# Windowed attention with global keys and a squared-ReLU MoE: attention cut into units that are placed between the steps of the MoE

## The chip, the cores and the metric

The kernel runs on one core of a Trainium2 chip. TensorE (PE; its weight loads are shown apart as PEld), VectorE (DVE), ScalarE (ACT), GpSimd (POOL) and SyncE (SP) each work through their own list of instructions in order and wait for each other by semaphores. DMA transfers are issued from POOL's and SP's lists and run beside them. The metric is device time in microseconds (us), the median of three runs.

## The reference

```python
# q, k, v: (4, 8, 768, 64), n_global = 8, n_local = 96; moe_w_in: (512, 2048), moe_w_out: (2048, 512)
scores = scale * np.matmul(q, k.transpose(0, 1, 3, 2))
rel = pos[:, None] - pos[None, :]
is_global = pos[None, :] < int(n_global)
is_local = (rel >= 0) & (rel < int(n_local))
keep = is_global | is_local
dist = np.where(is_global & ~is_local, float(n_local), np.abs(rel).astype(np.float32))
bias = -slopes[:, None, None] * dist[None, :, :]
scores = np.where(keep, scores + bias[None, :, :, :], -1000000000.0)
a = softmax(scores)          # over the keys
x = np.matmul(a, v)          # (4, 8, 768, 64), then laid out as 3072 tokens x 512
h = x @ w_in
r = np.maximum(h, 0.0)
out = (r * r) @ w_out        # (3072, 512), float32
```

A query of tile t (128 tokens) thus sees keys of its own tile, of the tile to the left, and the first eight keys of its batch.

## The kernel before

It has two stages, one after the other, and a scheduler of the tile framework orders each engine's list within them. All inputs are float32 in memory; POOL's DMA issues turn them into bfloat16 on the way.

*Attention* (L155 to L257) runs over 4 batches and 4 pairs of heads. For a pair, q and k of 768 tokens are loaded in four transfers (L164, L168; 128 partitions x 6 x 64 elements), transposed by PE in 128x128 blocks (L176, L181) and copied out of PSUM by DVE (L188, L189). For each head v is loaded (L198) and given a column of ones by POOL (L202). For each of six query tiles up to three 128x128 key blocks are multiplied (L218): the first tile of the batch for its global keys, the left tile and the own one. ACT takes the exponential of up to 384 columns (L228), DVE multiplies by a table of exponentiated biases, which is zero where a key is masked (L235), PE multiplies by v with its ones (L239: 64 outputs and the sum of the row), and DVE takes the reciprocal of the sum (L249) and scales (L250) into `x_sbuf`, which keeps all 3072 tokens.

*The MoE* (L259 to L318) starts when the attention pools are closed. It runs over 6 blocks of 512 tokens: PE transposes x (L278), DVE copies it (L284), and for each of 16 chunks of 128 hidden columns PE makes four matmuls of 512 columns (L290, stage 1), ACT the ReLU (L299), DVE the square (L301), PE four matmuls of 512 columns (L303, stage 2). ACT copies the sums out (L314), SP stores them (L315). Both weights come in one transfer each (L138, L143), issued ahead of q and k. [...]

Of the kernel before, what the change touches and what calls it, by code (L numbers as in the profile page):

```python
# [12 lines left out]
FP32 = mybir.dt.float32  # L14
BF16 = mybir.dt.bfloat16


@with_exitstack
def kernel(
# [26 lines left out]
    Act = mybir.ActivationFunctionType  # L46

    consts = ctx.enter_context(tc.tile_pool(name="consts", bufs=1))

    ident = consts.tile([128, 128], BF16)  # L50
    make_identity(nc, ident)

    def build_local_prebT(dst, offset):
        nc.gpsimd.iota(
            dst.bitcast(mybir.dt.int32),
            pattern=[[-1, 128]],
            base=-offset,
            channel_multiplier=1,
        )
# [31 lines left out]
    def build_prebT(offset, include_global, global_only, name):
        dst = consts.tile([128, 128], FP32, name=name, tag=name)
        if global_only:
            nc.gpsimd.memset(dst, float(-n_local))
            mask_globalT(dst)
        else:
            build_local_prebT(dst, offset)
            if include_global:
                gt = consts.tile([128, 128], FP32, name="gtT", tag="gtT")
                nc.gpsimd.memset(gt, float(-n_local))  # L100
                mask_globalT(gt)
                nc.vector.tensor_max(dst, dst, gt)
        return dst

    pbT_Br0 = build_prebT(0, True, False, "pbT_Br0")
    pbT_Ar128 = build_prebT(128, True, False, "pbT_Ar128")
    pbT_B = build_prebT(0, False, False, "pbT_B")
    pbT_G = build_prebT(0, False, True, "pbT_G")
    pbT_A = build_prebT(128, False, False, "pbT_A")

    pbT_cfg = [
        [pbT_Br0],
        [pbT_Ar128, pbT_B],
        [pbT_G, pbT_A, pbT_B],
    ]

    expBT = []
    for h in range(H):
        row = []
        for cfg in range(3):  # L120
            blocks = pbT_cfg[cfg]
            nb = len(blocks)
            eb = consts.tile(
                [128, nb * 128], BF16, name=f"eT_{h}_{cfg}", tag=f"eT_{h}_{cfg}"
            )
            for bi, pb in enumerate(blocks):
                nc.scalar.activation(
                    eb[:, bi * 128 : (bi + 1) * 128],
                    pb,
                    Act.Exp,  # L130
                    scale=float(slopes[h]),
                )
            row.append(eb)
        expBT.append(row)

    KM = d_model // 128
    w_in_sbuf = consts.tile([128, KM, d_ff], BF16)
    nc.gpsimd.dma_start(  # L138
        out=w_in_sbuf, in_=moe_w_in.rearrange("(km p) f -> p km f", p=128)
    )  # L140
    KF = d_ff // 128
    w_out_sbuf = consts.tile([128, KF, d_model], BF16)
    nc.gpsimd.dma_start(  # L143
        out=w_out_sbuf, in_=moe_w_out.rearrange("(kf p) f -> p kf f", p=128)
    )

    N_BT = B * N_ROW_TILES
    x_sbuf = consts.tile([128, N_BT, H, D], BF16)

    attn_ctx = ctx.enter_context(ExitStack())  # L150
    qkv_pool = attn_ctx.enter_context(tc.tile_pool(name="qkv", bufs=2))
    tqk = attn_ctx.enter_context(tc.tile_pool(name="tqk", bufs=2))
    work = attn_ctx.enter_context(tc.tile_pool(name="work", bufs=3))
    scalar_pool = attn_ctx.enter_context(tc.tile_pool(name="sc", bufs=4))
    psum_tr = attn_ctx.enter_context(tc.tile_pool(name="psumtr", bufs=1, space=bass.MemoryType.PSUM))  # L155
    psum_pool = attn_ctx.enter_context(tc.tile_pool(name="psum", bufs=3, space=bass.MemoryType.PSUM))
    psum_out = attn_ctx.enter_context(tc.tile_pool(name="psumo", bufs=3, space=bass.MemoryType.PSUM))

    for b in range(B):
        for kp in range(H // 2):  # L160
            q_b = qkv_pool.tile([128, N_ROW_TILES, 128], BF16, tag="q_b")
            k_b = qkv_pool.tile([128, N_ROW_TILES, 128], BF16, tag="k_b")
            for hh in range(2):
                nc.gpsimd.dma_start(  # L164
                    out=q_b[:, :, hh * D : (hh + 1) * D],
                    in_=q[b, 2 * kp + hh, :, :].rearrange("(t p) d -> p t d", p=128),
                )
                nc.gpsimd.dma_start(  # L168
                    out=k_b[:, :, hh * D : (hh + 1) * D],
                    in_=k[b, 2 * kp + hh, :, :].rearrange("(t p) d -> p t d", p=128),  # L170
                )
# [181 lines left out]
```

## Time and profile before

| | us |
|---|---|
| median of 3 runs | 407.82 (407.51 to 430.92) |
| span of the profiled execution | 406.0 |
| PE busy | 329.8 (81%) |
| DVE busy | 199.7 (49%) |
| ACT busy | 161.1 (40%) |
| POOL busy | 89.3 (22%) |

The span runs from the first to the last instruction of one profiled execution, whose own time is not listed apart from those of the runs. A busy time is the union of an engine's instructions; durations of matmuls are modelled from start to drain, so successive ones overlap, and what one costs in a row of them is the distance of their starts. Idle time counts only on the engine that the others wait for.

### The profile page before, as it was taken

What the parts mean: (1) busy time and instruction counts of PE and PEld (TensorE: products, weight loads), DVE (VectorE), ACT (ScalarE), POOL (GpSimd) and SP (SyncE); (2) the same over time, 40 slices, a digit from 0 to 9 for tenths busy, and PEclk for the clock granted to TensorE, in tenths of its full rate; (3) what the DMA queues carried; (4) which work ended last, traced back from release to release, by engine and by line L of the source; (5) the groups of instructions that cost most, each with busy time, mean ns of one, the idle gap of its engine ahead of it and who ended that gap; (6) DMA issues with size and microseconds to landing.
All of it is one profiled execution on the core that took longest, in us unless ns stands there. A gap on an engine that the chain in (4) does not pass through costs nothing.

```text
span 406.0 us, 5757 instructions
## 1 busy us (share of the span) xinstructions
PE 329.8 (81%) x1999; PEld 165.1 (41%) x2016; DVE 199.7 (49%) x712; ACT 161.1 (40%) x361; POOL 89.3 (22%) x158
## 2 busy tenths in 40 slices
PE   0008888888888888888897998999999999999991
PEld 0005544444555444444453334444434444434430
DVE  0004776776666777676763444335335335345240
ACT  6403444444544444443451334335235235235232
POOL 9316634544543443531100000000000000000000
PEclk9999999999999999999999999999999999999998
DMA  3999998899777879853310002001102002002002
GB/s 53 200 193 111 75 57 56 52 61 58 49 46 50 52 51 61 56 32 21 22 10 0 2 0 101 4 0 61 44 0 79 26 1 97 9 2 103 0 2 103
DMA packets 81341, 20.30 MB, mean 50 GB/s; under 512 B 75680, under 2 KB 77728, under 8 KB 81312
## 3 DMA queue, kind: packets, MB, share of 16 engines
q0 software_dynamic: 77856, 13.64, 42.6%
q1 hardware_dynamic: 3456, 6.29, 4.1%
q8 instruction: 16, 0.26, 0.3%
q14 instruction: 13, 0.11, 0.1%
HBM read 27.26 MB, written 6.29 MB: 83 GB/s over the span
## 4 chain that ended last, share of the span: by engine, by line
PE 73%; DVE 14%; DMA 6%; issue 2%; POOL 2%; ACT 2%; DVEq 0%; POOLq 0%; ACTq 0%
PE ps_out L303 21%; PE hT_ps L290 20%; PE sc_ps L218 15%; PE out_ps L239 9%; DMA q_b<-in_q_dram 5%; DVE attnT L235 4%; PE kT_ps L181 4%; PE qT_ps L176 4%; DVE x_sbuf L250 3%; DVE rsum L249 2%; DVE kT L189 2%; DVE xT L284 1%; DMA out_dram<-out_tile 1%; DVE h_sq L301 1%; ACT h_relu L299 1%
## 5 line engine op out<-in xcount | busy, mean ns | idle before, releaser
L228 ACT ACTIVATE esc<-sc_ps 128x384 bf16<-128x384 f32 (+1 forms) x192 | 81.1, 437 | 117.0 <-PE sc_ps L218 80.0
L301 DVE TENSOR_TENSOR h_sq<-h_relu 128x512 bf16<-128x512 f32 x96 | 66.3, 693 | 108.4 <-ACT h_relu L299 108.4
L299 ACT ACTIVATE h_relu<-hT_ps 128x512 f32<-128x512 f32 x96 | 57.1, 601 | 108.9 <-PE hT_ps L290 102.5
L290 PE MATMUL hT_ps<-xT,w_in_sbuf 128*128 128x512 bf16 x372 | 91.1, 386 | 4.3 <-DVE xT L284 3.1
L303 PE MATMUL ps_out<-w_out_sbuf,h_sq 128*128 128x512 bf16 x379 | 90.3, 381 | 4.2 <-DVE h_sq L301 3.7
L218 PE MATMUL sc_ps<-qT,kT 64*128 64x128 bf16 x480 | 81.5, 301 | 5.8 <-DVE kT L189 5.8
L239 PE MATMUL out_ps<-vS,attnT 128*128 128x65 bf16 x480 | 62.6, 244 | 23.6 <-DVE attnT L235 21.3
L235 DVE TENSOR_TENSOR attnT<-esc,eT 128x384 bf16<-128x384 bf16 (+1 forms) x192 | 59.7, 311 | 4.3 <-ACT esc L228 1.0
L290 PEld LDWEIGHTS <-w_in_sbuf 128*128 128x128 bf16 x384 | 37.6, 99 | 51.2 <-issue 4.7
L249 DVE RECIPROCAL rsum<-out_ps 128x1 f32<-128x1 f32 x192 | 31.9, 166 | 51.7 <-PE out_ps L239 50.6
L239 PEld LDWEIGHTS <-attnT 128*128 128x128 bf16 x480 | 36.9, 123 | 47.7 <-DVE attnT L235 41.4
L303 PEld LDWEIGHTS <-h_sq 128*128 128x128 bf16 x384 | 31.9, 98 | 57.6 <-DVE h_sq L301 28.1
L218 PEld LDWEIGHTS <-kT 64*128 64x128 bf16 x480 | 39.9, 121 | 25.4 <-DVE kT L189 8.3
L250 DVE TENSOR_SCALAR x_sbuf<-out_ps,rsum 128x64 bf16<-128x64 f32 x192 | 49.3, 277 | 0.1
L176 PE MATMUL qT_ps<-ident,q_b 128*128 128x128 bf16 x96 | 18.5, 302 | 31.3 <-DMA q_b<-in_q_dram 31.0
L168 POOL DMA_DIRECT2D k_b<-in_k_dram x32 | 26.3, 824 | 35.1 <-PE out_ps L239 22.1
L198 POOL DMA_DIRECT2D vS<-in_v_dram x32 | 26.5, 829 | 16.0 <-POOL vS L202 7.7
L164 POOL DMA_DIRECT2D q_b<-in_q_dram x32 | 26.3, 824 | 16.1 <-PE out_ps L239 9.4
L176 PEld LDWEIGHTS <-q_b 128*128 128x128 bf16 x96 | 8.0, 120 | 38.6 <-issue 37.1
L188 DVE COPY qT<-qT_ps 128x768 bf16<-128x768 bf16 x16 | 8.7, 542 | 28.0 <-PE qT_ps L176 28.0
L181 PE MATMUL kT_ps<-ident,k_b 128*128 128x128 bf16 x96 | 22.1, 296 | 0.0
L314 ACT COPY out_tile<-ps_out 128x512 f32<-128x512 f32 x24 | 13.1, 590 | 12.8 <-PE ps_out L303 11.1
(42 smaller groups left out, 69.1 us busy)
## 6 DMA issues: line engine op xcount, KB each, us to landing
out_dram<-out_tile SPq DMA_DIRECT2D x24, 256.0 KB, 2.0
q_b<-in_q_dram POOLq DMA_DIRECT2D x32, 96.0 KB, 3.3
k_b<-in_k_dram POOLq DMA_DIRECT2D x32, 96.0 KB, 3.2
vS<-in_v_dram POOLq DMA_DIRECT2D x32, 96.0 KB, 3.2
w_in_sbuf<-in_moe_w_in_dram POOLq DMA_DIRECT2D x1, 2048.0 KB, 12.8
w_out_sbuf<-in_moe_w_out_dram POOLq DMA_DIRECT2D x1, 2048.0 KB, 22.5
```

Of the source, the lines that this page charges most:

```text
L176: nc.tensor.transpose(out=qT_ps[:, t * 128 : (t + 1) * 128], in_=q_b[:, t, :], identity=ident,)
L181: nc.tensor.transpose(out=kT_ps[:, t * 128 : (t + 1) * 128], in_=k_b[:, t, :], identity=ident,)
L218: nc.tensor.matmul(out=sc_ps[:, bi * 128 : (bi + 1) * 128], lhsT=kT[:, kb * 128 : (kb + 1) * 128], rhs=qT[:, r : r + 128], start=True, sto ...
L228: nc.scalar.activation(out=esc[:, :ncols], in_=sc_ps[:, :ncols], func=Act.Exp, scale=scale,)
L235: nc.vector.tensor_mul(attnT[:, :ncols], esc[:, :ncols], expBT[h][cfg])
L239: nc.tensor.matmul(out=out_ps, lhsT=attnT[:, 128 * bi : 128 * (bi + 1)], rhs=vS[:, kb, :], start=(bi == 0), stop=(bi == nblk - 1), skip_gr ...
L249: nc.vector.reciprocal(rsum, out_ps[:, D : D + 1])
L250: nc.vector.tensor_scalar(out=x_sbuf[:, b * N_ROW_TILES + t, h, :], in0=out_ps[:, :D], scalar1=rsum, scalar2=None, op0=mybir.AluOpType.mult,)
L290: nc.tensor.matmul(out=hT_ps, lhsT=w_in_sbuf[:, kt, c * 128 : (c + 1) * 128], rhs=xT[:, kt, :], start=(kt == 0), stop=(kt == KM - 1), skip ...
L299: nc.scalar.activation(h_relu, hT_ps, Act.Relu)
L301: nc.vector.tensor_mul(h_sq, h_relu, h_relu)
L303: nc.tensor.matmul(out=ps_out[:, sub, :], lhsT=h_sq[:, sub * 128 : (sub + 1) * 128], rhs=w_out_sbuf[:, c, :], start=(c == 0), stop=(c == C ...
```

## The change

Nearly the whole body is written anew, and the order of each engine's list is now the order of the code (`manual_schedule`).

Data: q, k and v are loaded per 128-token tile for all eight heads (three transfers of 128x8x64 elements for each of 24 tiles), each into a buffer of its own; the weights in eight steps of 256 hidden columns. Six tiles and all weights are issued before the first unit of work, later tiles one per four steps. The first global keys no longer have a block of their own: POOL copies the eight global columns of `kT`, and the eight global rows of `v`, into the key tile to the left, once that tile has been used as an own tile. This works since with 96 local keys the first eight of the left tile are out of any local window.

Attention of one tile is cut into units: A (8 transposes of q and k, three DVE copies, q into zeroed halves so that a matmul has 128 rows and makes two heads at once), B and C (scores of two pairs of heads each: four matmuls of 256 columns, one exponential and one product of 1024 columns), D and E (16 matmuls with v in all, one reciprocal and one scaling of 256 columns for four heads), F (four transposes of x and a copy). The MoE runs over 12 blocks of 256 tokens in eight steps each: eight matmuls of 256 columns in stage 1, four of 512 in stage 2, the latter two steps later. Units of tiles 0 and 1 and the first four of tile 2 stand ahead of the first step; from then on one tile takes four steps: E of the one before and A, then B, then F of the one before and C, then D.

```diff
@@ setup: constants, tiles, loads @@
...
+    NSTEP = KF // 2
+    NBLK = NT // 2
+    work = ctx.enter_context(tc.tile_pool(name="work", bufs=2))
+    ps_acc = ctx.enter_context(tc.tile_pool(name="ps_acc", bufs=1, space=PSUM))
+    ps_h = ctx.enter_context(tc.tile_pool(name="ps_h", bufs=2, space=PSUM))
+    ps_sc = ctx.enter_context(tc.tile_pool(name="ps_sc", bufs=1, space=PSUM))
+    ps_tr = ctx.enter_context(tc.tile_pool(name="ps_tr", bufs=1, space=PSUM))
+    ps_o = ctx.enter_context(tc.tile_pool(name="ps_o", bufs=1, space=PSUM))
+    ctx.enter_context(tc.manual_schedule())
...
+    kT = [const([P, NPAIR, P], BF16, f"kT_{j}") for j in range(NT)]
+    NQZ = 3
+    qz = [const([P, NPAIR, 2, P], BF16, f"qz_{i}") for i in range(NQZ)]
+    w_in_sb = [const([P, KM, 2 * P], BF16, f"win_{s}") for s in range(NSTEP)]
+    w_out_sb = [const([P, 2, d_model], BF16, f"wout_{s}") for s in range(NSTEP)]
...
+    def load_tile(j):
+        b, t = divmod(j, TPB)
+        rows = slice(t * P, (t + 1) * P)
+        for dst, src in ((q_sb[j], q), (k_sb[j], k)):
+            nc.gpsimd.dma_start(
+                out=dst.rearrange("p (h d) -> p h d", h=H),
+                in_=src[b, :, rows, :].rearrange("h p d -> p h d"),
+            )
+        nc.gpsimd.dma_start(
+            out=v_sb[j][:, :, :D], in_=v[b, :, rows, :].rearrange("h p d -> p h d")
+        )
+    def load_weights(s):
+        f = slice(s * 2 * P, (s + 1) * 2 * P)
+        nc.gpsimd.dma_start(
+            out=w_in_sb[s], in_=moe_w_in[:, f].rearrange("(km p) f -> p km f", p=P)
+        )
+        nc.gpsimd.dma_start(
+            out=w_out_sb[s], in_=moe_w_out[f, :].rearrange("(c p) m -> p c m", p=P)
...
+    for j in range(NT):
+        nc.vector.memset(v_sb[j][:, :, D : D + 1], 1.0)
+    load_tile(0)
+    make_identity(nc, ident)
+    for i in range(NQZ):
+        nc.vector.memset(qz[i].bitcast(I32), 0)
+    load_tile(1)
...
+    nc.gpsimd.tensor_copy(pb0, pb[:, 0, :])
+    nc.gpsimd.tensor_scalar_max(
+        pb0[:n_global, :], pb0[:n_global, :], float(-n_local)
+    )
+    nc.gpsimd.memset(pb[:n_global, 1, :], float(-n_local))
...
+    for s in range(NSTEP):
+        load_weights(s)
+        if s % 2 == 1 and 2 + s // 2 < NT:
+            load_tile(2 + s // 2)
+    next_load = [2 + NSTEP // 2]
@@ attention, in six units per 128-token tile @@
...
+    def unit_a(j):
+        tr = ps_tr.tile([P, 2 * NPAIR, P], BF16, name="tr", tag="tr")
+        for pair in range(NPAIR):
+            c = slice(pair * P, (pair + 1) * P)
+            nc.tensor.transpose(out=tr[:, pair, :], in_=q_sb[j][:, c], identity=ident)
+        for pair in range(NPAIR):
+            c = slice(pair * P, (pair + 1) * P)
+            nc.tensor.transpose(
+                out=tr[:, NPAIR + pair, :], in_=k_sb[j][:, c], identity=ident
+            )
+        z = qz[j % NQZ]
+        nc.vector.tensor_copy(z[:D, :, 0, :], tr[:D, :NPAIR, :])
+        nc.vector.tensor_copy(z[D:, :, 1, :], tr[D:, :NPAIR, :])
+        nc.vector.tensor_copy(kT[j], tr[:, NPAIR:, :])
+    def globals_k(j):
+        if 1 <= j % TPB < TPB - 1:
+            g = kT[j - j % TPB]
+            nc.gpsimd.tensor_copy(kT[j][:, :, :n_global], g[:, :, :n_global])
+    def globals_v(j):
+        if 1 <= j % TPB < TPB - 1:
+            g = v_sb[j - j % TPB]
+            nc.gpsimd.tensor_copy(v_sb[j][:n_global], g[:n_global])
+    def unit_scores(j, hf):
+        z = qz[j % NQZ]
+        sc = ps_sc.tile([P, 2, 4 * P], FP32, name="sc", tag="sc")
+        first = j % TPB == 0
...
+            for pi in range(2):
+                pair = 2 * hf + pi
+                for i, kj in enumerate((j, j - 1)):
+                    nc.tensor.matmul(
+                        out=sc[:, pi, i * 2 * P : (i + 1) * 2 * P],
+                        lhsT=kT[kj][:, pair, :],
+                        rhs=z[:, pair, :, :],
+                        start=True,
+                        stop=True,
+                        skip_group_check=True,
+                    )
+        esc = work.tile([P, 8 * P], BF16, name="esc", tag="esc")
+        nc.scalar.activation(
+            out=esc, in_=sc.rearrange("p a b -> p (a b)"), func=Act.Exp, scale=scale
+        )
+        at = work.tile([P, 8 * P], BF16, name="at", tag="at", bufs=3)
...
+        if first or hf == 1:
+            globals_k(j)
+    def unit_pv(j, hf):
...
+                for i, kj in enumerate((j, j - 1)):
+                    nc.tensor.matmul(
+                        out=po[:, hi, :],
+                        lhsT=a4[:, hi // 2, i, hi % 2, :],
+                        rhs=v_sb[kj][:, h, :],
+                        start=(i == 0),
+                        stop=(i == 1),
+                        skip_group_check=True,
+                    )
+        rs = work.tile([P, 4, 1], FP32, name="rs", tag="rs")
+        nc.vector.reciprocal(rs, po[:, :, D : D + 1])
+        nc.vector.tensor_tensor(
+            out=x[:, 4 * hf : 4 * hf + 4, :],
+            in0=po[:, :, :D],
+            in1=rs.to_broadcast([P, 4, D]),
+            op=Alu.mult,
+        )
+        if hf == 1:
+            globals_v(j)
+    def unit_f(j):
+        x = attn.pop((j, "x")).rearrange("p h d -> p (h d)")
+        blk, tt = divmod(j, 2)
+        if tt == 0:
+            xT[blk] = work.tile([P, KM, 2 * P], BF16, name="xT", tag="xT")
+        trx = ps_tr.tile([P, KM, P], BF16, name="trx", tag="tr")
+        for kt in range(KM):
+            nc.tensor.transpose(
+                out=trx[:, kt, :], in_=x[:, kt * P : (kt + 1) * P], identity=ident
+            )
+        nc.vector.tensor_copy(xT[blk][:, :, tt * P : (tt + 1) * P], trx)
@@ the MoE in steps of 256 tokens and 256 hidden columns @@
...
+    def stage1(g):
+        blk, s = divmod(g, NSTEP)
+        hT = ps_h.tile([P, 2, 2 * P], FP32, name="hT", tag="hT")
+        for c in range(2):
+            for kt in range(KM):
+                nc.tensor.matmul(
+                    out=hT[:, c, :],
+                    lhsT=w_in_sb[s][:, kt, c * P : (c + 1) * P],
+                    rhs=xT[blk][:, kt, :],
+                    start=(kt == 0),
+                    stop=(kt == KM - 1),
+                    skip_group_check=True,
+                )
+        hr = work.tile([P, 2, 2 * P], FP32, name="hr", tag="hr")
+        nc.scalar.activation(hr, hT, Act.Relu)
+        hs = work.tile([P, 2, 2 * P], BF16, name="hs", tag="hs", bufs=4)
+        nc.vector.tensor_mul(hs, hr, hr)
+        hsq[g] = hs
+    def stage2(g):
+        blk, s = divmod(g, NSTEP)
+        hs = hsq.pop(g)
+        if s == 0:
+            acc[blk] = [
+                ps_acc.tile([P, d_model], FP32, name=f"acc{sub}", tag=f"acc{sub}")
+                for sub in range(2)
+            ]
+        for sub in range(2):
+            for c in range(2):
+                nc.tensor.matmul(
+                    out=acc[blk][sub],
+                    lhsT=hs[:, c, sub * P : (sub + 1) * P],
+                    rhs=w_out_sb[s][:, c, :],
+                    start=(s == 0 and c == 0),
+                    stop=(s == NSTEP - 1 and c == 1),
+                    skip_group_check=True,
+                )
+        if s == NSTEP - 1:
+            for sub in range(2):
+                o = work.tile([P, d_model], FP32, name="o", tag="o", bufs=4)
+                nc.scalar.copy(o, acc[blk][sub])
+                r = (blk * 2 + sub) * P
+                nc.sync.dma_start(out=out[r : r + P, :], in_=o)
@@ the fixed order @@
...
+    LEAD = 4
+    OFF = {"A": 0, "B": 1, "C": 2, "D": 3, "E": 4, "F": 6}
+    when = []
+    for j in range(NT):
+        for u, off in OFF.items():
+            if u == "C" and j % TPB == 0:
+                continue
+            if j == 0:
+                at_ = {"A": -100, "B": -98, "D": -96, "E": -95, "F": -93}[u]
+            elif j == 1:
+                at_ = {"A": -99, "B": -97, "C": -95.5, "D": -94, "E": -92, "F": -91}[u]
+            else:
+                at_ = 4 * (j - 2) - LEAD + off
+            when.append((at_, j, u))
+    when.sort()
+    pos = 0
+    DELAY = 2
+    NG = NBLK * NSTEP
+    for g in range(-1, NG + DELAY):
+        if 0 <= g < NG:
+            stage1(g)
+        while pos < len(when) and when[pos][0] <= g:
+            _, j, u = when[pos]
+            UNITS[u](j)
+            pos += 1
+        if g >= 0 and g % 4 == 0 and next_load[0] < NT:
+            load_tile(next_load[0])
+            next_load[0] += 1
+        if g - DELAY >= 0:
+            stage2(g - DELAY)
```

POOL's list at the end of its first loads. Before, the list goes on with loads and the ones of `vS`:

```order
L168 DMA k_b<-in_k_dram 128x6x64
L198 DMA vS<-in_v_dram 128x6x64 x2
L164 DMA q_b<-in_q_dram 128x6x64 [waits DMASW0_49]
L168 DMA k_b<-in_k_dram 128x6x64 [waits DMASW1_49]
L164 DMA q_b<-in_q_dram 128x6x64 [waits DMASW2_49]
L202 MEMSET vS 128x6 [waits DMASW6_49]
```

Now, the last of the 34 first loads (step 7 of the weights, tile 5), and what follows:

```order
L99 DMA wout_7_192<-in_moe_w_out_dram 128x2x512 [waits DMASW6_49]
L86 DMA q_5_83<-in_q_dram 128x8x64 [waits DMASW7_49]
L86 DMA k_5_107<-in_k_dram 128x8x64 [waits DMASW0_49]
L90 DMA v_5_131<-in_v_dram 128x8x64 [waits DMASW1_49,DVE_49]
L164 COPY kT_1_151<-kT_0_150 128x4x8 [waits DVE_49,PE_49]
L169 COPY v_1_127<-v_0_126 8x520 [waits PE_49]
```

[...]

PE's list where tile 2 is scored, ahead of the first MoE matmul, and the first of those a few rows on (kT_1 is the left tile, win_0 the first step's weights):

```order
L189 LDWEIGHTS kT_2_152 [waits DVE_49]
L189 MATMUL sc_418<-qz_2_176,kT_2_152 128x256 [waits Activation_49]
L189 LDWEIGHTS kT_1_151 [waits Pool_49]
L189 MATMUL sc_418<-qz_2_176,kT_1_151 128x256
...
L284 LDWEIGHTS win_0_177 [waits DMASW6_49]
L284 MATMUL hT_450<-xT_380,win_0_177 128x256
```

Before, scores follow the multiplication by v of an earlier head, and no MoE matmul stands near:

```order
L239 LDWEIGHTS attnT_2779
L239 MATMUL out_ps_2781<-vS_2701,attnT_2779 128x65
L218 LDWEIGHTS kT2_2809 [waits DVE_49]
L218 MATMUL sc_ps_2815<-qT2_2808,kT2_2809 128x128 [waits Activation_49]
L218 LDWEIGHTS kT2_2809
L218 MATMUL sc_ps_2826<-qT2_2808,kT2_2809 128x128 [waits Activation_49]
```

A wait for POOL has come into PE's list, and stage 1 behind it. DVE's list in a step that holds E and A, before and now:

```order
L188 COPY qT_234<-qT_ps 128x768 [waits PE_49]
L189 COPY kT_235<-kT_ps 128x768 [waits PE_49]
L235 TENSOR_TENSOR attnT<-esc,eT_0_116 128x128 [waits Activation_49]
L235 TENSOR_TENSOR attnT<-esc,eT_1_118 128x256 [waits Activation_49]
L249 RECIPROCAL rsum<-out_ps 128x1 [waits PE_49]
L250 TENSOR_SCALAR x_sbuf<-out_ps,rsum 128x64 [waits DVE_49]
```

```order
L295 TENSOR_TENSOR hs_590<-hr_588 128x512 [waits Activation_49]
L244 RECIPROCAL rs_601<-po_592 128x4 [waits PE_49]
L245 TENSOR_TENSOR x_562<-po_592,rs_601 128x256 [waits DVE_49]
L157 COPY qz_1_175<-tr_605 64x4x128 [waits PE_49]
L158 COPY qz_1_175<-tr_605 64x4x128
L159 COPY kT_4_154<-tr_605 128x512
L295 TENSOR_TENSOR hs_635<-hr_633 128x512 [waits Activation_49]
L207 TENSOR_TENSOR at_644<-esc_642,E_194 128x1024 [waits Activation_49]
```

The copies of q and k that the next step's scores need now stand behind the MoE's square and the scaling of the tile before.

## Rows read from the trace of the kernel before

**Rows 1.** The page: busy time of each engine.

```profile
PE 329.8 (81%) x1999; PEld 165.1 (41%) x2016; DVE 199.7 (49%) x712; ACT 161.1 (40%) x361; POOL 89.3 (22%) x158
```

**Rows 2.** The page: chain that ended last, by engine.

```profile
PE 73%; DVE 14%; DMA 6%; issue 2%; POOL 2%; ACT 2%; DVEq 0%; POOLq 0%; ACTq 0%
```

**Rows 3.** Stretches: length, busy time (and instructions) by engine, granted clock, DMA.

```profile
core 0: us, PE busy (x) PEld busy (x) DVE busy (x) ACT busy (x) POOL busy (x), PEclk, DMA share, GB/s
100.00:120.00 20.00, 17.04 (x132) 10.22 (x132) 13.40 (x64) 8.73 (x21) 8.06 (x14) 1.00 0.78 50
300.00:400.00 100.00, 94.98 (x458) 40.30 (x464) 39.97 (x56) 37.76 (x67) 0.00 (x0) 1.00 0.09 32
```

**Rows 4.** Timeline, PE in attention: start, length, instruction, count [idle before].

```profile
31.01 0.69 PE L176 MATMUL qT_ps<-ident,q_b 128*128 128x128 bf16 x5 [31.01 <-DMA q_b<-in_q_dram]
33.55 1.14 PE L218 MATMUL sc_ps<-qT,kT 64*128 64x128 bf16 x9 [1.01 <-DVE kT L189]
...
101.18 0.35 PE L239 MATMUL out_ps<-vS,attnT 128*128 128x65 bf16 x3 [0.52 <-DVE attnT L235]
```

**Rows 5.** Timeline, PE in the MoE.

```profile
216.62 4.05 PE L290 MATMUL hT_ps<-xT,w_in_sbuf 128*128 128x512 bf16 x9 [0.22 <-issue]
222.48 1.89 PE L290 MATMUL hT_ps<-xT,w_in_sbuf 128*128 128x512 bf16 x8
...
247.21 0.61 PE L278 MATMUL xTp<-ident,x_sbuf 128*128 128x128 bf16 x8
249.13 3.29 PE L290 MATMUL hT_ps<-xT,w_in_sbuf 128*128 128x512 bf16 x13 [1.32 <-DVE xT L284]
```

**Rows 6.** Timeline, POOL's issues of loads at the start.

```profile
5.30 0.89 POOL L138 DMA_DIRECT2D w_in_sbuf<-in_moe_w_in_dram  x1
18.38 0.82 POOL L164 DMA_DIRECT2D q_b<-in_q_dram  x1 [5.36 <-DMA w_in_sbuf<-in_moe_w_in_dram]
29.23 0.82 POOL L168 DMA_DIRECT2D k_b<-in_k_dram  x1 [10.03 <-DMA w_out_sbuf<-in_moe_w_out_dram]
```

**Rows 7.** Stretches at the start (last column GB/s): w_in; w_out; q and k.

```profile
14.00:16.00 2.00, 0.00 (x0) 0.00 (x0) 0.00 (x0) 0.27 (x2) 0.00 (x0) 1.00 1.07 217
26.00:28.00 2.00, 0.00 (x0) 0.00 (x0) 0.00 (x0) 0.00 (x0) 0.00 (x0) 1.00 1.24 206
30.00:34.00 4.00, 1.98 (x17) 1.57 (x18) 1.02 (x2) 0.12 (x1) 2.44 (x6) 1.00 2.41 153
```

**Rows 8.** Groups by shape: count, busy us, mean ns of one, idle before.

```profile
L228 ACT ACTIVATE esc<-sc_ps 128x384 bf16<-128x384 f32 x128 | 62.0, 490 | 46.7 <-DVE attnT L235 31.5 <-PE sc_ps L218 15.2
L249 DVE RECIPROCAL rsum<-out_ps 128x1 f32<-128x1 f32 x192 | 31.9, 166 | 51.7 <-PE out_ps L239 50.6
L228 ACT ACTIVATE esc<-sc_ps 128x256 bf16<-128x256 f32 x32 | 12.3, 383 | 9.0 <-PE sc_ps L218 6.3 <-DVE attnT L235 1.6 <-PE qT_ps L176 1.1
L250 DVE TENSOR_SCALAR x_sbuf<-out_ps,rsum 128x64 bf16<-128x64 f32 x192 | 49.3, 277 | 0.1
L188 DVE COPY qT<-qT_ps 128x768 bf16<-128x768 bf16 x16 | 8.7, 542 | 28.0 <-PE qT_ps L176 28.0
L284 DVE COPY xT<-xTp 128x2048 bf16<-128x2048 bf16 x6 | 7.3, 1220 | 1.8 <-PE xTp L278 1.6 <-issue 0.2
```

**Rows 9.** Chain in order of time, two neighbouring groups of the MoE.

```profile
222.64 1.73 PE hT_ps L290 x8
224.37 1.80 PE ps_out L303 x8
```

**Rows 10.** Timeline: a relu and its square, and the last output copies.

```profile
393.04 0.60 ACT L299 ACTIVATE h_relu<-hT_ps 128x512 f32<-128x512 f32 x1 [2.07 <-PE hT_ps L290]
393.67 0.69 DVE L301 TENSOR_TENSOR h_sq<-h_relu 128x512 bf16<-128x512 f32 x1 [1.98 <-ACT h_relu L299]
...
399.03 1.07 ACT L314 COPY out_tile<-ps_out 128x512 f32<-128x512 f32 x2 [1.85 <-PE ps_out L303]
...
401.73 1.26 ACT L314 COPY out_tile<-ps_out 128x512 f32<-128x512 f32 x2 [1.62 <-DMA out_dram<-out_tile]
```

More of the change, by code (lines that the diff above doesn't have):

```diff
@@ L15 @@
 BF16 = mybir.dt.bfloat16
+I32 = mybir.dt.int32
+Act = mybir.ActivationFunctionType
+Alu = mybir.AluOpType
+PSUM = bass.MemoryType.PSUM
 @with_exitstack
@@ L91, in build_prebT @@
[L91 to L124, printed above, removed]
-            )
[L126 to L157, printed above, removed]
@@ L270 @@
[L270 to L288 removed]
+            out=dst, in_=dst, compare_op=Alu.is_ge, fill=MASK_VAL,
@@ new lines, in globals_k @@
+    def globals_k(j):
[10 more added lines that the diff above has]
+        first = j % TPB == 0
+        if first:
+            for pair in range(NPAIR):
+                nc.tensor.matmul(
+                    out=sc[:, pair // 2, (pair % 2) * 2 * P : (pair % 2 + 1) * 2 * P],
+                    lhsT=kT[j][:, pair, :],
+                    rhs=z[:, pair, :, :],
[10 more added lines that the diff above has]
+                        lhsT=kT[kj][:, pair, :],
+                        rhs=z[:, pair, :, :],
+                        start=True,
+                        stop=True,
+                        skip_group_check=True,
[3 more added lines that the diff above has]
+            out=esc, in_=sc.rearrange("p a b -> p (a b)"), func=Act.Exp, scale=scale
+        )
+        at = work.tile([P, 8 * P], BF16, name="at", tag="at", bufs=3)
+        bias = (
+            E0.rearrange("p a b c -> p (a b c)")
+            if first
+            else E[:, 2 * hf : 2 * hf + 2].rearrange("p a i e c -> p (a i e c)")
+        )
+        nc.vector.tensor_mul(at, esc, bias)
+        attn[j, hf] = at
+        if first:
+            attn[j, 1] = at
+        if first or hf == 1:
+            globals_k(j)
@@ new lines, in unit_pv @@
+    def unit_pv(j, hf):
+        if hf == 0:
+            attn[j, "x"] = work.tile([P, H, D], BF16, name="x", tag="x")
+        x = attn[j, "x"]
+        first = j % TPB == 0
+        at = attn.pop((j, hf))
+        po = ps_o.tile([P, 4, D + 1], FP32, name="po", tag="po")
+        for hi in range(4):
+            h = 4 * hf + hi
+            if first:
+                nc.tensor.matmul(
+                    out=po[:, hi, :],
+                    lhsT=at[:, h * P : (h + 1) * P],
+                    rhs=v_sb[j][:, h, :],
+                    start=True,
+                    stop=True,
+                    skip_group_check=True,
+                )
+            else:
+                a4 = at.rearrange("p (a i e c) -> p a i e c", a=2, i=2, e=2)
+                for i, kj in enumerate((j, j - 1)):
+                    nc.tensor.matmul(
+                        out=po[:, hi, :],
+                        lhsT=a4[:, hi // 2, i, hi % 2, :],
[14 more added lines that the diff above has]
+            globals_v(j)
@@ L309 @@
                     skip_group_check=True,
                 )
-        for sub in range(SUB):
-            out_tile = moe_out.tile([128, d_model], FP32, tag="out_tile")
-            nc.scalar.copy(out_tile, ps_out[:, sub, :])
-            nc.sync.dma_start(
-                out=out[mt * R + sub * 128 : mt * R + (sub + 1) * 128, :], in_=out_tile
-            )
+        if s == NSTEP - 1:
[4 more added lines that the diff above has]
+                nc.sync.dma_start(out=out[r : r + P, :], in_=o)
```

206 lines of the change are left out of this document (42 added, 164 removed).

## Prediction, made before the changed kernel was run

> **What bounds the kernel now.** I read the page's busy line first: PE shows work in 329.8 of 406.0 us, every other engine in less than half [rows 1]. The chain that ended last says the same: 73% of it is PE, 14% DVE, 6% DMA [rows 2]. But an average over stages hides that there are three of them. The table of stretches shows attention with PE 17.04, DVE 13.40 and ACT 8.73 of 20 us, and the MoE with PE at 95 of 100 us and DVE at 40 [rows 3]. The timelines give the limits: the first transposes start at 31.01 us, released by a DMA; the first long run of MoE matmuls starts at 216.62, one of them about 0.8 earlier; the copies behind the last start at 399.03 [rows 4, 5, 10]. So: 31 us of loading, 185 of attention, 183 of MoE, 7 of tail.
>
> The spacing of matmuls then tells why attention is long. A merged row of n matmuls lasts (n-1) spacings and one modelled duration (0.28, 0.24, 0.22 and 0.38 us for the four kinds that follow). In attention, nine score matmuls of 128 columns take 1.14 us, so (1.14-0.28)/8 = 107 ns, and three of 65 columns 0.35, so 55 ns. In the MoE, eight 128-column transposes take 0.61 us, (0.61-0.22)/7 = 56 ns, and eight 512-column matmuls (1.89-0.38)/7 = 216 ns [rows 4, 5]. [...] The granted-clock column reads 1.00 in both stretches [rows 3], so it doesn't show this step; I go by spacing. At the start of the MoE nine matmuls took 4.05 us ((4.05-0.38)/8 = 459 ns), later ones 216 [rows 5]: the level rose after some 4.6 us of unbroken matmuls. In attention the small PE groups wait on DVE and ACT (PE idle 0.52 us before a group of three [rows 4]), and the level stays low.
>
> **What the change does, and the sum.** Attention's 185 us stop being a stage of their own: their PE work goes between MoE matmuls, while ACT and DVE do the softmax under those matmuls. I sum PE's time, since PE then runs in one fixed order.
>
> *Start.* POOL issues all 34 first loads before its first copy of global keys (kT_1), and PE waits for that copy in the scores of tile 2, ahead of the first MoE matmul. A load issue costs POOL about 0.85 us (0.82, 0.89); only eight may be out, the ninth waiting for the first to land (POOL idled 5.36 and 10.03 us on w_in and w_out) [rows 6]. Six tile loads and the constants take POOL 6x0.85+3.6 = 8.7 us; w_in of step 0 is issued by 9.6, and data come about 2.4 us later (before: issued by 6.2, 2.1 MB landed at 18.4 at 217 GB/s, so started near 8.6). From 12.0 us the queue is full. Rates: 153 GB/s where pieces are 64 elements, 206 for w_out's 512, 217 for w_in's 2048 [rows 7]; w_in's new 256-element pieces lie between 153 and 206, I take 185. A tile of 0.39 MB takes 2.57 us, a weight step 0.26/0.185+0.26/0.206 = 2.7. Eight steps and four tiles are 31.9 us. The last issue (v of tile 5) waits for k of tile 4, behind which 0.86+5.4+2.57 = 8.8 us remain: 12.0+31.9-8.8 = 35.1, issue to 35.9, the copy to 36.2. Bounds: POOL's own 34x0.85+5 = 34 below, all pieces at 153 GB/s 39 above. Then tile 2 runs alone on PE: scores 0.85 and 0.3 to their end, exp 1.0 (384 columns take 490 ns, 256 take 383, so 1024 about 1.03 [rows 8]) since the score buffer is single, second scores 0.85, PV 0.45: 39.7 us when stage 1 starts.
>
> *PE work after that*, at the higher level's spacings: stage 1, 768 matmuls of 256 columns x 0.108 = 82.9; stage 2, 384x0.216 = 82.9; scores, 156x0.108 = 16.8 (four for a batch's first tile, eight for others); q, k and x transposes 256x0.056 = 14.3; PV 320. No row has 65 columns at the higher level: below, 55 ns; above, 107, what a 128-column pair takes at the lower level. I take 56, since transposes load the same 128x128 weights and keep 56. 17.9. Sum 214.8. [...]
>
> *Changeovers.* A pair of eight-matmul groups in the MoE repeats every 1.73+1.80 = 3.53 us [rows 9], 16x0.216 = 3.46, so 0.037 per change of group. Four steps have 14 changes, 0.52 us per tile, 22 tiles: 11.4.
>
> *The added wait.* Transposes of q and k come in one step, the scores that need their three copies in the next. Per step DVE squares first: stage 1 ends at 0.87, relu starts 0.2 later and takes 0.63 to the square's start (393.04, 393.67 [rows 10]), so at 1.70. Then square 0.61, reciprocal and scaling 0.6 (166 ns, and 277+192x1.06 = 480 for 256 columns of f32, at twice the copies' time per column), three copies. A bf16 copy of 768 columns takes 542 ns, one of 2048 takes 1220 [rows 8], so 0.53 ns a column, and 0.41 us for 512, 0.33 each back to back. The last is visible at 4.03. PE is there at 0.87+0.45+0.45 (PV, transposes)+0.88+0.87 = 3.53. PE waits 0.5 us, in 21 tiles 10.5. Behind it stands stage 2 of that step, and nothing else can pass. Low bound 0 (if PE is late anyway), high bound with 0.69 per copy below.
>
> *Hidden.* ACT per tile: 4 relu 2.4, 2 exp 2.05, copies of the output 0.6: 5.1 of 10 us. DVE: 4 squares 2.8, 2 masks 1.4 (bf16, at the copies' rate), 2 scalings 1.3, 4 copies 1.6: 7.1 of 10. Tile loads 2.6 us of DMA per 10. POOL three issues 2.6 and two small copies, done well before the next scores. A load is asked for twelve steps ahead. Were ACT's cover gone, 1.03 us of exp would show twice per tile.
>
> *Level and tail.* The first steps run at the lower level, as the MoE's first 4.6 us did: half of that, 2.3, and first steps without stage 2 wait 0.7 longer: 3. Tail: before, the last group ends at 398.99, two copies 1.07, and from the last copy's end 402.99 to 406.0 it is 3.0 [rows 10]; two copies now: 4.2.
>
> 39.7+214.8+11.4+10.5+3.0+4.2 = 283.6 us span. The profiled span of before is 406.0, the median 407.8, so 1.8 outside: **285 us**.
>
> **Rivals.**
> 1. *DVE's round is longer.* If 512-column copies cost what a 512-column f32 product does (0.69 us [rows 10]) and scaling too, the scores' wait is 0.5+3x0.28+0.2 = 1.5 us per tile: +21, **306**. For it: the copies write strided halves on 64 partitions, which no row shows. Against: the copies of before, also from PSUM, take 0.53 ns a column.
> 2. *Weight loads pace the small matmuls.* At 107 ns for all transposes and PV, 576x0.051 = +29: **314**. Against: 56 ns in the MoE's transposes. [...]
> 3. *All handovers hidden*, PE late enough that copies are ready, and loads at 206 GB/s: -10.5-4 and half the changeovers: **265**.
> [...]
>
> **How the numbers follow.** Forecast (265 to 297 by its own bounds) 0.58; DVE 0.16; weight loads 0.10; all hidden 0.10; low level 0.06. The range of 8 in 10 reaches from 264 to 314. A change under about 2% could not be told from none here. Faster by over 2%: 0.93 (the first four, with 0.01 taken off for mishaps); within 2%: 0.01; slower: 0.06.
>
> **What would show it.** Right: PE idle until about 36 us, ended by POOL's copy of kT_1; stage 1 starting near 40; then steps of 2.3 to 2.6 us; 512-column spacings of 216 ns; a wait of PE for DVE's copy of kT (about 0.5 us, once per four steps); POOL with two or three microseconds of issues per ten. Wrong: stage 1 near 20 us (then POOL's copies don't hold it); mask or relu as releaser of PE in most steps; 427 ns spacings past the first steps; a DMA as releaser after 50 us.

## The result, and the profile of the changed kernel

The changed kernel takes **280.9 us** (280.8 to 281.1) where the kernel before takes 407.7: a ratio of 0.689 (0.688 to 0.691). One of the four runs of the kernel before (430.9 us) was in a slow state and is left out of the ratio. The forecast was 285.0 in a range of 264 to 314. The profiled execution has a span of 279.3 us where 283.6 were summed.

The page's busy lines and the chain by engine and by line (answering to [rows 1, 2]):

```profile
PE 226.2 (81%) x1935; PEld 156.0 (56%) x1968; DVE 161.7 (58%) x359; ACT 117.4 (42%) x181; POOL 92.0 (33%) x137
...
PE 59%; DVE 19%; POOL 6%; DMA 6%; ACT 5%; issue 3%; ACTq 0%; POOLq 0%
PE hT L284 24%; PE acc L308 23%; PE sc L189 7%; DVE hs L295 6%; ACT hr L293 5%; DVE kT L159 3%; DVE qz L158 3%; DVE x L245 3%; DMA win<-in_moe_w_in_dram 3%; DMA wout<-in_moe_w_out_dram 3%; DVE qz L157 2%; PE po L235 2%; PE trx L261 2%; POOL q L86 1%; POOL k L86 1%
```

PE's share is 81% as before; its busy time fell by 104 us. The stretches (columns as in [rows 3]) show one stage in place of two:

```profile
30.00:40.00 10.00, 0.54 (x3) 0.42 (x4) 0.00 (x0) 0.00 (x0) 7.59 (x11) 1.00 1.64 189
100.00:150.00 50.00, 45.91 (x405) 31.88 (x411) 33.26 (x70) 23.88 (x36) 15.47 (x21) 1.00 0.69 67
250.00:279.00 29.00, 25.33 (x182) 16.67 (x184) 11.65 (x21) 10.36 (x18) 0.00 (x0) 1.00 0.13 49
```

From 100 us on PE, DVE and ACT work together (46, 33 and 24 of 50 us); in 30 to 40 us hardly anything but POOL's issues and the loads runs. PE's list of waits (line waited for, us, times, longest) names what is left:

```profile
PE sc L189 <- DVE kT L159: 15.8, 19, 1.4
PE sc L189 <- POOL kT L164: 11.6, 1, 11.6
PE tr L150 <- DMA q<-in_q_dram: 6.8, 2, 5.0
PE sc L189 <- ACT esc L198: 6.5, 3, 4.5
PE po L235 <- DVE x L245: 2.3, 3, 1.7
```

The first two are the two waits that the prediction put a price on: scores behind DVE's copies, and POOL's copy behind the loads. The other three lie ahead of 45 us. The timeline of the start, lines of POOL and PE:

```profile
38.31 0.87 POOL L90 DMA_DIRECT2D v<-in_v_dram  x1 [0.18 <-issue]
39.18 0.22 POOL L164 COPY kT<-kT 128x32 bf16<-128x32 bf16 x1
...
39.46 0.82 PE L189 MATMUL sc<-qz,kT 128*128 128x256 bf16 x3 [11.65 <-POOL kT L164]
...
42.65 1.90 PE L284 MATMUL hT<-xT,win 128*128 128x256 bf16 x8
44.79 0.42 PE L235 MATMUL po<-v,at 128*128 128x65 bf16 x8 [0.24 <-DVE x L245]
...
45.49 1.04 PE L284 MATMUL hT<-xT,win 128*128 128x256 bf16 x8
```

PE stands still until POOL has issued tile 5's v; the first eight stage-1 matmuls take 1.90 us, the next eight 1.04, the same step as in [rows 5]. The level rose between these two: from 42.65 on the matmuls are still 0.22 us apart ((1.90-0.82)/5, with the three of the same shape at 39.46), and the eight PV matmuls at 44.79 (0.42 us, where the eight at 42.20 took 0.64) are at the higher level already, that of 0.108 us for 256 columns; PE's work had begun again at 39.46. One step of the loop, from stage 1 through E and A, and the next one up to the scores that wait (lines of PE and POOL, and of DVE from 152.48 on):

```profile
151.94 1.04 PE L284 MATMUL hT<-xT,win 128*128 128x256 bf16 x8
152.48 0.42 DVE L245 TENSOR_TENSOR x<-po,rs 128x256 bf16<-128x256 f32 x1
152.96 0.42 PE L235 MATMUL po<-v,at 128*128 128x65 bf16 x8
153.22 0.39 PE L150 MATMUL tr<-ident,q 128*128 128x128 bf16 x4
153.41 0.61 POOL L169 COPY v<-v 8x520 bf16<-8x520 bf16 x1 [3.98 <-PE po L235]
153.44 0.39 PE L153 MATMUL tr<-ident,k 128*128 128x128 bf16 x4
153.65 0.92 DVE L295 TENSOR_TENSOR hs<-hr 128x512 bf16<-128x512 f32 x1 [0.74 <-ACT hr L293]
153.88 0.81 PE L308 MATMUL acc<-wout,hs 128*128 128x512 bf16 x3
154.49 0.17 DVE L244 RECIPROCAL rs<-po 128x4 f32<-128x4 f32 x1
154.53 1.04 PE L284 MATMUL hT<-xT,win 128*128 128x256 bf16 x8
154.70 0.42 DVE L245 TENSOR_TENSOR x<-po,rs 128x256 bf16<-128x256 f32 x1
155.04 0.41 DVE L157 COPY qz<-tr 64x512 bf16<-64x512 bf16 x1
155.46 0.43 DVE L158 COPY qz<-tr 64x512 bf16<-64x512 bf16 x1
155.90 0.42 DVE L159 COPY kT<-tr 128x512 bf16<-128x512 bf16 x1
156.38 0.61 PE L189 MATMUL sc<-qz,kT 128*128 128x256 bf16 x4 [0.81 <-DVE kT L159]
```

Eight stage-1 matmuls of 0.108 us from 154.53 are over at 155.39, so PE loses 0.99 us to 156.38; the 0.81 shown leave out the drain of the last matmul. In the six tiles without a copy of v on POOL beside the square the idle time shown is 0.58, so 0.75 in all. (Of the four stage-2 matmuls at 153.88 the trace has three.) A tile repeats every 10.13 us (these scores come again at 166.50), 2.53 per step. And at the end, where no units are left, steps repeat every 1.74 us:

```profile
264.96 1.04 PE L284 MATMUL hT<-xT,win 128*128 128x256 bf16 x8
...
266.70 1.04 PE L284 MATMUL hT<-xT,win 128*128 128x256 bf16 x8
...
268.44 1.04 PE L284 MATMUL hT<-xT,win 128*128 128x256 bf16 x8
```

That is 8x0.108+4x0.216 = 1.73: changing groups costs nothing there, unlike in [rows 9].

### The profile page after: what moved, and what is told of

It is laid out like the page before. It is cut to its first block, busy times and chain, and to the rows that moved or that the text cites. A ratio compares the mean times of both kernels' runs of the same rounds, so it can differ in the third digit from the quotient of the medians.

```text
span 279.3 us, 4817 instructions
## 1 busy us (share of the span) xinstructions
PE 226.2 (81%) x1935; PEld 156.0 (56%) x1968; DVE 161.7 (58%) x359; ACT 117.4 (42%) x181; POOL 92.0 (33%) x137
## 4 chain that ended last, share of the span: by engine, by line
PE 59%; DVE 19%; POOL 6%; DMA 6%; ACT 5%; issue 3%; ACTq 0%; POOLq 0%
PE hT L284 24%; PE acc L308 23%; PE sc L189 7%; DVE hs L295 6%; ACT hr L293 5%; DVE kT L159 3%; DVE qz L158 3%; DVE x L245 3%; DMA win<-in_moe_w_in_dram 3%; DMA wout<-in_moe_w_out_dram 3%; DVE qz L157 2%; PE po L235 2%; PE trx L261 2%; POOL q L86 1%; POOL k L86 1%
## 5 line engine op out<-in xcount | busy, mean ns | idle before, releaser
L293 ACT ACTIVATE hr<-hT 128x512 f32<-128x512 f32 x96 | 57.6, 600 | 107.2 <-PE hT L284 107.2
L295 DVE TENSOR_TENSOR hs<-hr 128x512 bf16<-128x512 f32 x96 | 69.7, 726 | 55.5 <-ACT hr L293 54.7
L284 PE MATMUL hT<-xT,win 128*128 128x256 bf16 x768 | 100.4, 274 | 0.2
L308 PE MATMUL acc<-wout,hs 128*128 128x512 bf16 x351 | 92.9, 379 | 1.5
L284 PEld LDWEIGHTS <-win 128*128 128x128 bf16 x768 | 75.4, 98 | 28.8
L198 ACT ACTIVATE esc<-sc 128x1024 bf16<-128x1024 f32 x44 | 45.0, 1024 | 40.6 <-PE sc L189 38.4
L207 DVE TENSOR_TENSOR at<-esc,E 128x1024 bf16<-128x1024 bf16 x44 | 30.3, 689 | 45.2 <-ACT esc L198 44.8
L189 PE MATMUL sc<-qz,kT 128*128 128x256 bf16 x160 | 26.0, 287 | 33.9 <-DVE kT L159 15.8
L308 PEld LDWEIGHTS <-hs 128*128 128x128 bf16 x384 | 35.0, 98 | 24.2 <-DVE hs L295 0.2
L90 POOL DMA_DIRECT2D v<-in_v_dram x24 | 21.8, 909 | 0.5 <-issue 0.2
```

Source lines behind the costliest of these rows:

```text
L90: nc.gpsimd.dma_start(out=v_sb[j][:, :, :D], in_=v[b, :, rows, :].rearrange("h p d -> p h d"))
L189: nc.tensor.matmul(out=sc[:, pi, i * 2 * P : (i + 1) * 2 * P], lhsT=kT[kj][:, pair, :], rhs=z[:, pair, :, :], start=True, stop=True, skip_ ...
L198: nc.scalar.activation(out=esc, in_=sc.rearrange("p a b -> p (a b)"), func=Act.Exp, scale=scale)
L207: nc.vector.tensor_mul(at, esc, bias)
L284: nc.tensor.matmul(out=hT[:, c, :], lhsT=w_in_sb[s][:, kt, c * P : (c + 1) * P], rhs=xT[blk][:, kt, :], start=(kt == 0), stop=(kt == KM - ...
L293: nc.scalar.activation(hr, hT, Act.Relu)
```

## The experiments

All edits are to the changed kernel (280.9 us).

**Unit A one step earlier.**

```diff
-    OFF = {"A": 0, "B": 1, "C": 2, "D": 3, "E": 4, "F": 6}
+    OFF = {"A": -1, "B": 1, "C": 2, "D": 3, "E": 4, "F": 6}
```

> The changed kernel with one number other: unit A (transposes of q and k with their three DVE copies) stands one step earlier, so two steps lie between it and the scores that need its copies. Theory 1 (the copies come late, behind the MoE's square and the scaling on DVE; the trace of the changed kernel shows PE idle 0.82 us before the scores in 14 tiles and 0.58 in 5, to which some 0.17 of drain belongs): this wait goes away whole, 21 tiles x 0.9 to 1.0, so 261 us (257 to 266). Rival 1 (the size of the prediction, 0.5 us per tile): 270. Rival 2 (DVE's round of four steps is what PE really waits for, so the wait moves to the PV matmuls or to stage 2): 276 or more.

Measured 258.1 us (257.4 to 258.8), 22.8 less. PE's waits on DVE's copies are down to one of 1.4 us, in the prologue:

```profile
PE sc L189 <- POOL kT L164: 11.4, 1, 11.4
...
PE sc L189 <- DVE kT L159: 1.4, 1, 1.4
```

Theory 1 holds, and the 0.5 us of the prediction was half of what the wait cost. The same three copies on the same engine cost nothing when a step lies between; DVE is not full. The saving is a little more than 21x0.95 = 20 since the short wait of E for the scaling (152.96 in place of 152.80 above, 0.16 us in 20 tiles) went too: in this run E's matmuls follow stage 1 at once (starts at 157.31 and 156.43, eight matmuls of 0.108 us apart).

**The first batch's global copies on DVE.**

```diff
-            nc.gpsimd.tensor_copy(kT[j][:, :, :n_global], g[:, :, :n_global])
+            eng = nc.vector if j < TPB else nc.gpsimd
+            eng.tensor_copy(kT[j][:, :, :n_global], g[:, :, :n_global])
...
-            nc.gpsimd.tensor_copy(v_sb[j][:n_global], g[:n_global])
+            eng = nc.vector if j < TPB else nc.gpsimd
+            eng.tensor_copy(v_sb[j][:n_global], g[:n_global])
```

> The changed kernel with the copies of global keys and values of the first batch on DVE instead of POOL, so that they don't stand behind POOL's 34 first loads. Theory 1 (the start is held by these copies alone): tile 2's scores start at about 27.4 us in place of 39.5 and stage 1 near 31 in place of 42.7; the weights of later steps land in time; 269 us (266 to 272). Rival (loading is what holds the start: the weights' steps and tiles 3 to 5 then stop PE in the first eight steps): PE waits for DMA between 31 and 45 us, and the time stays at 276 or more.

Measured 269.9 us (269.7 to 270.1), 11.1 less. From PE's timeline:

```profile
27.49 1.04 PE L191 MATMUL sc<-qz,kT 128*128 128x256 bf16 x4 [1.39 <-DVE kT L159]
...
30.90 1.90 PE L286 MATMUL hT<-xT,win 128*128 128x256 bf16 x8
```

Stage 1 starts at 30.90, 11.75 us earlier, and PE's waits hold no DMA after that. The queue position of two small copies cost 11 us, not the loading itself.

**The copies of v on ACT.**

```diff
-            nc.gpsimd.tensor_copy(v_sb[j][:n_global], g[:n_global])
+            nc.scalar.copy(v_sb[j][:n_global], g[:n_global])
```

> The changed kernel with the copies of the eight global rows of v on ACT instead of POOL. In the changed kernel's trace the square that runs beside such a copy takes 0.93 us in place of 0.69, and the wait before the scores is 0.82 in those tiles and 0.58 in the others. Theory 1 (POOL's copy slows DVE's product beside it): all squares take 0.69, all such waits 0.58, 15 tiles x 0.24 = 3.6 us less: 277.3 us (276.3 to 278.5). Rival (what slows it is POOL's loads that follow at once, or the place in the program): no change, 280 to 282.

Measured 277.8 us (277.5 to 278.0), 3.2 less (277.78 after 280.94). The square in the same step (DVE's timeline) is back at its own length, as in [rows 10], and PE's wait (list of waits) has shrunk from 15.8 to 12.0 us:

```profile
151.84 0.69 DVE L295 TENSOR_TENSOR hs<-hr 128x512 bf16<-128x512 f32 x1 [0.74 <-ACT hr L293]
```

```profile
PE sc L189 <- DVE kT L159: 12.0, 19, 1.4
```

So a POOL copy of eight partitions slowed the DVE product beside it by 0.24 us, and each time on the way to the scores. It did so 14 times, not the 15 of the expectation: in tile 3 the product began just ahead of POOL's copy and kept its 0.69 us (lines in the last section). POOL's load issues that follow it are still there and do no such harm.

**Attention first, then the MoE**, in the same units and steps.

```diff
-            xT[blk] = work.tile([P, KM, 2 * P], BF16, name="xT", tag="xT")
+            xT[blk] = work.tile([P, KM, 2 * P], BF16, name="xT", tag="xT", bufs=NBLK)
...
-        while pos < len(when) and when[pos][0] <= g:
+        while pos < len(when):
             _, j, u = when[pos]
             UNITS[u](j)
+            if u == "E" and j >= 1 and next_load[0] < NT:
+                load_tile(next_load[0])
+                next_load[0] += 1
```

> The changed kernel's units and steps, but not interleaved: all units of attention run first in their order, then all steps of the MoE (x of all blocks is kept; loads follow one tile per tile). It tells how much of the gain is the interleaving and how much the batching of heads and the folding of global keys. Theory 1 (interleaving is most of it): the start as in the changed kernel, 43 us; attention at the lower TensorE level, a tile per 7.8 us by its chain (scores 0.85 and 0.3, exp 1.05, second scores 1.15, exp 1.05, mask 0.7, PV and transposes 1.35, copies 1.3), 21 tiles 164; MoE 96 steps of 1.735, 167; tail 6: 380 us (350 to 400). Rival (the batching did it): attention at 4 us per tile, 300 us or less.

Measured 391.9 us (two runs, 390.8 and 392.9): 12 more than expected, and only 4% less than the kernel before. Attention runs until 217 us, 8.4 us for a usual tile. Its stretch, and lines of the timeline (PE, one of DVE) in it and in the MoE behind it:

```profile
60.00:180.00 120.00, 62.00 (x504) 45.35 (x504) 59.56 (x147) 27.02 (x27) 46.41 (x63) 1.00 0.78 50
```

```profile
127.66 1.04 PE L189 MATMUL sc<-qz,kT 128*128 128x256 bf16 x4 [1.39 <-DVE kT L159]
...
132.73 0.42 DVE L245 TENSOR_TENSOR x<-po,rs 128x256 bf16<-128x256 f32 x1
133.21 0.62 PE L235 MATMUL po<-v,at 128*128 128x65 bf16 x8 [1.95 <-DVE x L245]
...
217.18 3.94 PE L284 MATMUL hT<-xT,win 128*128 128x256 bf16 x24
```

No engine is busy for much more than half of the time: with one buffer for scores and one for PV, every engine waits for the next in a chain. The four scores take 1.04 us where they take 0.61 in the mixed loop (lower level), and E's eight PV matmuls wait 1.95 us for the scaling that frees their buffer. Most of these 1.95 us were in my 7.8 (the second exponential and its product, which starts at 131.91); left out were D's reciprocal and scaling, which stand behind that product on DVE (132.52 to 133.15), 0.6 us, and that is the difference between 8.4 and 7.8.

So of the 127 us gained, 111 come from the interleaving (391.9 to 280.9) and 16 from all the rest as it stands without it: batching of heads, folding of keys, new loads. The 16 are those of an order that has the mixed loop's single buffers; how batching alone does with more buffers was not run. Nor do the runs part what interleaving brings, hidden waits and the higher level. An estimate from the spacings of this run and of the mixed loop: the 36 PE matmuls of a tile (8 scores, 12 transposes, 16 PV) take 3.9 us at the lower level (0.214, 0.107, 0.056) and 2.0 at the higher (0.108, 0.057, 0.031), so over 21 tiles the level is worth 39 of the 111 us at most.

**The third key block put back as work.** For tiles two and later of a batch, each half gets this, and PV matmuls on `at3` ahead of its own:

```diff
+        third = j % TPB >= 2
+        if third:
+            for pi in range(2):
+                nc.tensor.matmul(
+                    out=sc[:, pi, 2 * P : 4 * P],
+                    lhsT=kT[j - 1][:, 2 * hf + pi, :],
+                    rhs=z[:, 2 * hf + pi, :, :],
...
+            nc.scalar.activation(out=esc3, in_=sc[:, 0, :], func=Act.Exp, scale=scale)
...
+            nc.vector.tensor_mul(at3, esc3, bias[:, : 4 * P])
```

> The changed kernel with the work of a third key block put back for the 16 tiles that had one before (third tile of a batch and later): per half two more score matmuls of 256 columns, an exponential and a product of 512 columns, four more PV matmuls; the added block is the left tile over again, and its PV sums are overwritten by the proper ones, so the extra work is work alone. It prices the folding of the global keys. Theory 1 (PE's list is the bound in these steps, other engines have room): 4x0.110+8x0.031 = 0.69 us per tile, 11 in all: 292 us (289 to 296). Rival 1 (it hides in the wait before the scores): 281 to 284. Rival 2 (ACT and DVE, with 1.2 and 0.8 us more per tile, become late): 300 or more.

Measured 291.6 us (291.4 to 292.2), 10.6 more (291.57 after 280.94), 0.66 us for each of 16 tiles. Theory 1 holds: in the mixed loop the added PE matmuls cost their own spacing, and the exponential and the product that ACT and DVE got per half cost nothing that shows. The folding of global keys spares about 11 us of PE's work. But it is what brought the small copies, and these cost more in the changed kernel: 11.1 us by the run with the first batch's copies on DVE and 3.2 by the one with the copies of v on ACT. By these runs, folding pays only with its copies moved; a kernel with neither folding nor copies was not run.

**Both edits together**: A one step earlier, and the first batch's copies on DVE.

> Both edits together: unit A one step earlier, and the first batch's global copies on DVE. Theory (the two waits are in different stretches and independent): the savings add, 280.9-22.8-11.1 = 247 us (245 to 250). Rival (with the loop faster and the start earlier, loads of weights and tiles become late): PE waits for DMA before 60 us, 252 or more.

Measured 246.8 us (245.7 to 247.0); the sum of the two savings gives 247.0. A ratio of 0.606 (0.605 to 0.607) to the kernel before, and the best version here. PE's list of waits is empty after 30 us, so the rival's waits for DMA did not come; the loop is PE's own work, 208.4 us from the first stage-1 matmul (31.73) to the end of the last matmul (240.15).

**And tile 2's units moved into steps 0 to 3.**

```diff
+            elif j == 2:
+                at_ = {"A": -5, "B": 0, "C": 1, "D": 1.5, "E": 2, "F": 3.5}[u]
+            elif j == 3 and u == "A":
+                at_ = 0
```

> Both edits of the run before, and tile 2's scores and PV moved from ahead of the first step into steps 0 to 3 (tile 3's transposes back into step 0), so that stage 1 need not wait for the chain scores, exponential, scores. Theory (3.4 us of that chain stood alone on PE; its matmuls, 1.3 us, stay): stage 1 starts near 27.5 us, 245 us (243.5 to 246.5) where the run before gives 247. Rival (the single score buffer makes the two tiles wait for each other in steps 0 to 2): no gain, 247 to 249.

Measured 248.5 us (248.0 to 249.9): a miss, and a little slower than 246.8. The rival's time came. Stage 1 does start earlier, at 25.88 us in place of 31.73, but the time is given back at once (the first line is of the run before):

```profile
31.73 1.53 PE L286 MATMUL hT<-xT,win 128*128 128x256 bf16 x8
...
25.88 1.91 PE L286 MATMUL hT<-xT,win 128*128 128x256 bf16 x8
...
29.62 0.61 PE L150 MATMUL tr<-ident,q 128*128 128x128 bf16 x4 [0.97 <-DMA q<-in_q_dram]
...
30.86 1.91 PE L286 MATMUL hT<-xT,win 128*128 128x256 bf16 x8
...
34.52 0.27 PE L191 MATMUL sc<-qz,kT 128*128 128x256 bf16 x1 [1.11 <-ACT esc L200]
...
38.83 0.42 PE L237 MATMUL po<-v,at 128*128 128x65 bf16 x8 [1.88 <-DVE x L247]
```

The score buffer that the rival named is one of three things that these lines show. Tile 3 has not landed when its transposes come up, the single score buffer makes C of tile 2 and B of tile 3 wait for each other, and the second step's matmuls still take 1.91 us, at the lower level. Tile 4's transposes start at 41.50 us, 3.05 later than in the run before (its profile is that of its longest run, 249.9 us).

## Why the prediction was right, step by step

**The mechanism.** PE's own list is what the loop waits for, the MoE runs at the higher level throughout, ACT and DVE hide. In the main it stands: steps without units take 1.74 us, the chain is PE for 59%, and the third block costs its PE spacing. DVE hides less than I said: 22.6 us of PE's waits are for it, twice the 10.5, and 19% of the chain is DVE. The sum of 283.6 missed by only 4.3 us, and that closeness is luck: four of its terms are off by 3 to 12 us and cancel:

| term | predicted us | measured us | from |
|---|---|---|---|
| until stage 1 starts | 39.7 | 42.65 | timeline |
| PE work | 214.8 | 206.8 | the same sum with PV at 31 ns, not 56 |
| changes of group | 11.4 | 0 | steps of 1.74 us |
| waits on DVE | 10.5 | 22.6 | 15 tiles at 0.99 (the first waits 0.4 more, which is left to the row below), 6 at 0.75, 20 times 0.16 for E; 22.8 by A one step earlier |
| lower level at the start | 3.0 | 3.5 | not measured: what is left of 232.9 in the loop (42.65 to the last matmul's end, 275.5) |
| tail | 4.2 | 3.8 | 279.3 less 275.5 |
| span | 283.6 | 279.3 | |

The PE work can be checked: the run with both edits has no waits in its loop and takes 208.4 us for it, with tile 3's transposes (0.5 us) ahead of it; 206.8-0.5 leave 2.1 for its first steps.

**The start.** The reason was right and shown by taking it away: POOL's two copies behind 34 issues held PE for 11.6 us. The size was 3 us short. The constants ended later (first weight load issued at 10.82 us in place of 8.7), and POOL came to the copy at 39.18, not 35.9. I had the DMA queue as what POOL waits for; between 10.82 and 39.18 it waited for landed loads and the like only some 6 us, and issuing 28 loads took it the other 22, so that without these waits it would have come to the copy at some 33 us, near my low bound of 34. The chain from the copy to stage 1 was right (3.47 us, 3.5 predicted).

**PV.** Eight matmuls of 65 columns take 0.41 us (three took 0.35 in [rows 4]), (0.41-0.195)/7 = 31 ns with the duration of one taken off, near 65/128 of the transposes' 57 ns (29 ns). I took 56 from the transposes on the belief that loading 128x128 weights sets the pace; it was the 128 columns. 320 of them make 8 us. Rival 2 falls: transposes keep 57 ns and PV takes 31.

**Changes of group.** The 0.037 us were read off the MoE before, where the chain alternated between 1.73 and 1.80 us. The new order has them not at all, at its end or in the mixed steps (stage 2, stage 1, PV and stage 2 start at 149.10, 149.96, 150.84 and 151.08, each the sum of its spacings after the one before, to 0.02 us). That a price per change holds in another order was argued, not shown, and it fell.

**The wait on DVE.** The place, the cause and the frequency were right; the size was half. From the end of stage 1 to the visible copy I had 3.16 us (4.03-0.87; the parts that I gave make 3.11); 152.81 to 156.38 is 3.57. Of the 0.41, 0.24 are the square slowed by POOL's copy, and the rest the copies: they follow each other at 0.42 to 0.44 us, with no overlap, where I took 0.33. PE came earlier by PV's smaller spacing (0.20), which is lost in the wait. Rival 1 was the right direction with the wrong reason: neither the copies (407 to 427 ns, 410 predicted) nor the scaling (424, 480 predicted) ran longer. The 480 rested on twice the copies' time per column, an estimate that no run shows: from 277 ns for 64 columns [rows 8] to 424 for 256 it is 0.77 ns a column.

**The level.** The low level (0.06 of the chances) didn't come: from 45.49 us on eight matmuls of 256 columns take 1.04 us, 0.108 each. The staged run shows the other side: the same units alone, with waits between them, stay at the lower level (four score matmuls take 1.04 us at 121.00 and 1.01 at 212.22, where they take 0.61 in the mixed loop).

## What to carry to other kernels

Work of a chain that crosses engines is well put between independent matmuls that keep PE's list full: taking that away gave back 111 of the 127 us here. In a hand-written order give each hand-over the time of its whole queue: a wait of 0.75 to 0.99 us per tile went when its producer moved by one step, and a copy of 0.2 us behind 34 load issues held the program for 11 us. Count with a saving the small work that it brings: the folding spared 11 us of PE's time and its copies cost some 14.
An estimate that comes out right can rest on terms that cancel, so price each term against its own row afterwards.

## What the runs showed of the hardware that I had not expected

A DVE product that reads f32 operands took 0.93 us in place of 0.69 when a POOL copy of 8x520 bf16 (0.61 us) had begun 0.23 to 0.24 us before it, and 0.69 with that copy on ACT. With A one step earlier the copy begins 0.39 us before the product, and the product takes 0.77. When the product came first, by 0.02 us, it kept its 0.69 and the copy took 1.14. Lines of the changed kernel (tile 3), then of the run with A one step earlier:

```profile
45.22 0.69 DVE L295 TENSOR_TENSOR hs<-hr 128x512 bf16<-128x512 f32 x1 [0.48 <-ACT hr L293]
45.24 1.14 POOL L169 COPY v<-v 8x520 bf16<-8x520 bf16 x1 [2.78 <-PE po L235]
...
151.20 0.61 POOL L169 COPY v<-v 8x520 bf16<-8x520 bf16 x1 [4.27 <-PE po L235]
151.59 0.77 DVE L295 TENSOR_TENSOR hs<-hr 128x512 bf16<-128x512 f32 x1
```

So the later of the two is held up: 0.24 us where 0.37 us of POOL's copy were left when the product began, 0.08 where 0.22 were left, in both cases 0.13 to 0.14 less than the rest of the copy. Why the two get in each other's way no run shows. POOL's DMA issues (0.9 us each) beside DVE's copies had no effect on these (0.40 to 0.43 us in tiles with and without them).

And weight loads of 128x128 did not show as time of their own: a pair of load and 65-column matmul follows the next at 31 ns, where 65/128 of the 57 ns of a 128-column pair are 29.
